# A fused attention and MLP kernel: q and k of batch 1 released by half of w_in's third quarter, w_out by the first 256 keys, and another searched order of all instructions

## The chip, the cores and the metric

The kernel runs on one core of a Trainium2 chip. The metric is the time of one execution on the device, in microseconds (us). A core has five engines with a stream of instructions each: TensorE (PE, matrix products; PEld are its weight loads), VectorE (DVE), ScalarE (ACT), GpSimd (POOL) and SyncE (SP, which here only issues transfers). Transfers (DMA) issued by SP, POOL and ACT run on 16 DMA engines that all queues share. Working memory is SBUF; matrix products land in PSUM, in 8 banks.

## The reference

```python
def _attn_ref(q, k, v, global_idx):          # q, k, v: 8 batches, 8 heads, 576 positions, 64
    scores = scale * np.matmul(q, k.transpose(0, 1, 3, 2))
    mask = np.abs(pos[:, None] - pos[None, :]) <= 32
    mask = mask | is_global[:, None] | is_global[None, :]      # 8 global positions
    scores = np.where(mask, scores, -1000000000.0)
    attn = np.exp(scores - np.max(scores, axis=-1, keepdims=True))
    return np.matmul(attn / (np.sum(attn, axis=-1, keepdims=True) + 1e-09), v)

def _moe_ref(x, w_in, w_out):                # 4608 tokens, 512 -> 2048 -> 512
    h = x @ w_in
    g = np.maximum(h, 0.0) + np.log1p(np.exp(-np.abs(h)))     # softplus
    return g @ w_out
```

The second function takes the first one's output, with the heads of a position side by side, as x.

## The kernel before

A batch's 576 positions are 18 blocks of 32. The unit of attention is a *pair* n (36 in all): four blocks of 32 queries, all 8 heads. A query block sees its own and the two neighbouring key blocks, and a slot with the 8 global keys. For pair n the steps are: scores `s` (L1085, 64 small matmuls), for the first four pairs on top of a mask that a full-size matmul puts into PSUM (L1068, L1078); row maximum `m` (L1100 or L1102, VectorE); exponential `st` (ScalarE, L1121 or L1125); sum and reciprocal `rs` (L1134, VectorE); multiplication `pn` (L1140, GpSimd or VectorE); transposition into `pt` (L1149, VectorE). The 8 global queries of a batch are computed apart: `sg` scores, `gm` and `gnb` maxima, `pg` exponential, `pgt` its transpose, `ov` values, `vg` the result.

Four pairs are a tile m of 512 tokens (9 tiles). Its values `xo` (L1259) are products of `pt` with `vb`; they are copied to `xT` (L728). Then `h` = xT times w_in (L1294, 16 column groups c of 128, 4 matmuls each), softplus `g` (L1300, ScalarE), and `o` = g times w_out (L1305), which is copied to `osb` and stored. The first tile's values come in three groups of 1, 2 and 1 pairs, the second tile's in two (1 and 3), so that h starts early on 128 and 256 columns.

Batches 0 and 1 come in naturally: for q and for k two *parts* of 256 positions (512 KB each) and a small part of 64 positions in two transfers. Each part is cast to bf16 (`qb`, `kb`), transposed on TensorE (`tr`, L865 or L868, with a product that picks the global rows, L871 or L875), and copied into `qx` and `kx`. Later batches are loaded in another layout and transposed on VectorE.

SP issues q, k and (from batch 1 on) v in one queue. POOL issues batch 0's v (8 transfers `vb`), w_in (`win`: four quarters, each in two halves of 64 partitions, 8 transfers), w_out (`wout`, 4 transfers) and the stores. Since SP's transfers would start at once, SP first issues a tiny transfer that reads one element of a weight tile, so that it waits until that weight has landed: `follow` (L761, tile `trail`). Ahead of batch 1's parts it reads the last partition of w_in's third quarter, which its second half brings. In the same way a one-column copy `seen` on GpSimd (L1373, L1437) holds w_in and w_out back until a part has landed.

The order of everything is set by a planner in the file, the class `_Order`. Each job has a cost per engine, dependencies, PSUM banks. The planner walks through `ORDER`, a table of numbers (job times 5 plus engine) that a search outside the file has found, and emits the jobs in the order of the times that its own model gives. This model also contains the fetching of TensorE's instructions in blocks (`BLOCK = 256`, asked for at instruction 130 and every 256 later, needed at 448 and every 256 later: `ASK`, `NEED`, `stall`), the DMA queues (`settle`), a price for going from one TensorE tile shape to another (`SWITCH`, job attribute `array`), and fills waits of TensorE in the first 34 us with matmuls that nobody reads (`keep`, `warm`, L737).

## Time and profile before

| what | value |
|---|---|
| three runs | 333.17, 333.18, 332.8 us; median 333.17 |
| the profiled execution | 331.16 us, its span on the core 329.1 us |
| mean granted TensorE clock | 0.995 |
| instructions in the span | 12101 |
| busy | PE 97%, PEld 52%, DVE 67%, ACT 71%, POOL 60% |
| chain that ended last | PE 90%; o 39%, h 37% |
| read / written from memory | 36.71 MB / 9.44 MB |

The profiled execution is one; its own time is 2 us under the median of the three. Busy shares are shares of the span; a matmul's end is modelled, so a busy PE is not PE at its peak. In a row of the order of time, the first number is the start in us from the span's start, the second the time from the first instruction's start to the last one's end, xN the number of instructions, and in brackets the idle time ahead of them with what ended it.

### The profile page before, as it was taken

The page shows a single profiled execution, that of the slowest core. Times are in us where ns is not written, and L with a number is a line of the kernel's source. Part 1 is how long each engine was busy: PE and PEld are TensorE (multiplying, and loading weights), DVE is VectorE, ACT ScalarE, POOL GpSimd, SP SyncE. Part 2 cuts the span into 40 slices and gives each one's busy share as a digit, 9 for nine tenths or more (in the row PEclk, how much of TensorE's full clock was granted, in tenths as well). Part 3 has the DMA queues.
Part 4 walks back from the last instruction along what each step waited for, and adds up shares of the span by engine and source line. Part 5 has one row for each costly group of instructions (what it writes and reads, how often), then busy time and mean ns, then how long its engine had stood idle before and what let it go on. Part 6 is the DMA issues. An engine that isn't in the chain of part 4 may idle for free.

```text
span 329.1 us, 12101 instructions
## 1 busy us (share of the span) xinstructions
PE 319.9 (97%) x5290; PEld 171.3 (52%) x5290; DVE 219.9 (67%) x386; ACT 233.8 (71%) x459; POOL 196.0 (60%) x175
## 2 busy tenths in 40 slices
PE   8878999999999999999999999999999999999996
PEld 3536876565555444544555445445544454454444
DVE  7796689847997799884995975378776970431000
ACT  5698879676798896488558857995749647914622
POOL 7827828996678567969587496738282927230000
PEclk9997999999999999999999999999999999999999
DMA  7998999999889899999999960370010012001002
GB/s 193 187 205 195 198 189 155 157 166 244 136 152 146 152 226 173 180 228 189 178 179 167 155 162 4 127 145 3 4 66 0 36 66 85 13 32 66 34 32 97
DMA packets 168796, 42.14 MB, mean 128 GB/s; under 512 B 153256, under 2 KB 165800, under 8 KB 168744
## 3 DMA queue, kind: packets, MB, share of 16 engines
q1 hardware_dynamic: 155928, 27.15, 46.8%
q0 software_dynamic: 10944, 11.08, 16.9%
q10 hardware_dynamic: 1872, 3.15, 2.5%
q8 instruction: 41, 0.67, 0.9%
q14 instruction: 11, 0.09, 0.1%
HBM read 36.71 MB, written 9.44 MB: 140 GB/s over the span
## 4 chain that ended last, share of the span: by engine, by line
PE 90%; DVE 2%; SPq 2%; DMA 2%; issue 1%; ACT 1%
PE o L1305 39%; PE h L1294 37%; PE xo L1259 4%; PE s L1085 4%; DMA stage<-in_q_dram 2%; PE ov L1005 2%; SPq L522 1%; PE pick L894 1%; SPq L526 1%; PE sg L976 1%; PE warm L737 1%; DVE qx L728 1%; PE tr L865 1%; DVE m L1100 1%; PE pick L907 1%
## 5 line engine op out<-in xcount | busy, mean ns | idle before, releaser
L1305 PE MATMUL o<-wout,g 128*128 128x512 bf16 (+1 forms) x592 | 138.3, 374 | 0.0
L1294 PE MATMUL h<-xT,win 128*128 128x512 bf16 (+3 forms) x768 | 137.8, 328 | 0.1
L1300 ACT ACTIVATE g<-h 128x512 bf16<-128x512 f32 (+3 forms) x192 | 84.5, 503 | 30.0 <-PE h L1294 27.0
L1140 POOL TENSOR_TENSOR pn<-st,rs 128x1024 bf16<-128x1024 f32 (+1 forms) x38 | 66.7, 1766 | 55.7 <-DVE rs L1134 49.9
L1294 PEld LDWEIGHTS <-win 128*128 128x128 bf16 x768 | 67.5, 99 | 59.6 <-issue 0.8
L1305 PEld LDWEIGHTS <-g 128*128 128x128 bf16 x592 | 55.9, 98 | 60.7 <-ACT g L1300 1.0
L1108 POOL TENSOR_TENSOR st<-st,m 128x1024 f32<-128x1024 f32 x32 | 60.2, 1894 | 27.1 <-DVE m L1102 27.0
L1089 DVE TENSOR_TENSOR st<-s,mask 128x512 f32<-128x512 f32 x64 | 41.1, 677 | 18.6 <-PE s L1085 18.4
L1132 DVE TENSOR_REDUCE sm<-st 128x8 f32<-128x1024 f32 x32 | 38.5, 1203 | 14.8 <-ACT st L1125 14.6
L1102 DVE TENSOR_REDUCE m<-st 128x8 f32<-128x1024 f32 x32 | 37.9, 1209 | 0.3
L728 ACT COPY osb<-o 128x512 f32<-128x512 f32 (+1 forms) x30 | 17.2, 577 | 22.6 <-PE o L1305 20.2
L1125 ACT ACTIVATE st<-st 128x1024 f32<-128x1024 f32 x32 | 32.7, 1052 | 0.3
L1149 DVE STREAM_TRANSPOSE pt<-pn 128x512 int32<-128x512 int32 x36 | 24.5, 690 | 5.2 <-POOL pn L1140 5.1
L728 ACT CAST xT<-xo 128x512 bf16<-128x512 f32 (+3 forms) x28 | 11.7, 467 | 18.8 <-PE xo L1259 18.8
L728 DVE CAST xT<-xo 128x512 bf16<-128x512 f32 (+3 forms) x20 | 11.3, 601 | 17.5 <-PE xo L1259 17.4
L1300 ACT ACT_TABLE_LOAD x15 | 19.2, 1283 | 1.7 <-PE h L1294 1.5
L1125 ACT ACT_TABLE_LOAD x14 | 18.0, 1283 | 0.7 <-ACT osb L728 0.4
L725 POOL TENSOR_SCALAR qb<-stage 128x1152 bf16<-128x1152 f32 (+2 forms) x15 | 16.8, 1126 | 2.2 <-issue 1.1
L1085 PE MATMUL s<-kx,qx 64*32 64x128 bf16 x1152 | 14.5, 220 | 3.6 <-issue 2.8
L1085 PEld LDWEIGHTS <-qx 64*32 64x32 bf16 x1152 | 10.4, 90 | 12.2 <-issue 8.9
L728 POOL CAST vb<-stage 128x1152 bf16<-128x1152 f32 x12 | 13.7, 1146 | 3.3 <-DMA stage<-in_v_dram 3.3
L737 PE MATMUL warm<-vb 128*128 128x512 bf16 x46 | 13.9, 451 | 1.3 <-DVE vb L559 1.3
(127 smaller groups left out, 287.2 us busy)
## 6 DMA issues: line engine op xcount, KB each, us to landing
stage<-in_v_dram SPq DMA_DIRECT2D x56, 144.0 KB, 4.2
stage<-in_q_dram SPq DMA_DIRECT2D x48, 144.0 KB, 3.7
stage<-in_k_dram SPq DMA_DIRECT2D x48, 144.0 KB, 4.0
out_dram<-osb POOLq DMA_DIRECT2D x24, 256.0 KB, 3.2
out_dram<-osb ACTq DMA_DIRECT2D x11, 256.0 KB, 2.0
stage<-in_q_dram SPq DMA_DIRECT2D x4, 512.0 KB, 6.2
stage<-in_k_dram SPq DMA_DIRECT2D x4, 512.0 KB, 6.9
win<-in_moe_w_in_dram POOLq DMA_DIRECT2D x8, 256.0 KB, 7.7
```

What stands on the lines that cost most here:

```text
L728: {"ACT": nc.scalar.copy, "DVE": V.tensor_copy, "POOL": nc.gpsimd.tensor_copy}[e](out, in_)
L1085: nc.tensor.matmul(out=PS["s", n, g][quad(a), x, :], lhsT=qx[b % 2][rows(g), a, j * BL:(j + 1) * BL], rhs=kx[b % 2][rows(g), a, e0 * BL:(e ...
L1089: V.tensor_tensor(out=PS["st", n][:, h, :, :], in0=PS["s", n, h][:, :, :], in1=mask[:, h, j0:j0 + PB, :, :].rearrange("p j s i -> p j (s i ...
L1102: V.reduce_max(out=m[:], in_=flat(PS["st", n], h0, h1), axis=AX)
L1108: on(e).tensor_tensor(out=t, in0=t, in1=over(PS["m", n, y][:], SL * BL), op=OP.subtract)
L1125: nc.scalar.activation(out=t, in_=t, func=AF.Exp)
L1132: V.reduce_sum(out=sm[:], in_=flat(PS["st", n], h0, h1), axis=AX)
L1140: on(e).tensor_tensor(out=PS["pn", n][:, :, :, h0:h1].rearrange("p x s h -> p h x s"), in0=PS["st", n][:, h0:h1], in1=PS["rs", n, y][:].re ...
L1149: V.transpose(out=bass.AP(base.tensor, base.offset, ap=[list(base.ap[0]), [2 * STEP, PB // 2], [STEP + BL // 2, 2], [1, SL * BL]]), in_=PS ...
L1294: nc.tensor.matmul(out=h[:, :], lhsT=w_in_t[c // 4][:, kd, c % 4 * P:(c % 4 + 1) * P], rhs=PS["xT", m][:, kd, lo:hi], start=(kd == 0), sto ...
L1300: nc.scalar.activation(out=PS["g", m, c][:, lo:hi], in_=PS[key][:, lo_of(c, hi - lo)], func=AF.Softplus)
L1305: nc.tensor.matmul(out=PS["o", m, ns, a][:, :], lhsT=PS["g", m, kf][:, ns * P:(ns + 1) * P], rhs=w_out_t[kf // 4][:, kf % 4, a:z], start=( ...
```

## The change

It has four parts. `follow` gets the row that it reads: for w_in row 0, which the first half of the third quarter brings, and batch 1's parts depend on that half alone. The `seen` copy ahead of w_out waits for the first 256 keys of batch 1, where it waited for the next 256. The hold times of w_in and w_out on GpSimd go (they only shift the planner's times). And the planner's constants are others (SWITCH, SLOW, BEGIN, the fills, the latency of a POOL transfer; `array` numbers that count the changes between the score, value and global shapes), with a table `ORDER` searched anew under them. Its rows tell a reader nothing; two stand here.

```diff
-    SWITCH = 107
+    SWITCH = 96
-    SLOW = ((27000, 8000), (34500, 6200), (55000, 8200), (230000, 6000), (1e9, 4500))
+    SLOW = ((27000, 6500), (36500, 5500), (50000, 7500), (230000, 5800), (1e9, 4500))
-                took_ = max(next(x for until, x in self.SLOW if ask < until), self.backlog(ask + 1200) - ask + 2400)
+                took_ = max(next(x for until, x in self.SLOW if ask < until), self.backlog(ask + 1400) - ask + 2400)
-    BEGIN = 3300
+    BEGIN = 2900
-                dma.append((mine, t + 1500 if j["cost"][e][0] else t, j["moves"], j))
+                dma.append((mine, t + (1900 if mine == "POOL" else 1500) if j["cost"][e][0] else t, j["moves"], j))
-    ORDER = (52, 57, 62, 162, 167, 122, 137, 146, 156, 4, 117, 113, 151, 141, 132, 127, 182, 172, 177, 187, 370, 9, 14, 213,
+    ORDER = (52, 156, 146, 113, 141, 151, 57, 162, 62, 167, 127, 9, 132, 137, 122, 4, 211, 215, 226, 258, 243, 245, 260, 230,
...
-    def follow(x, t):
+    def follow(x, t, row):
-        nc.sync.dma_start(out=trail[x:x + 1, :], in_=t[D:D + 1, t.shape[1] - 1, t.shape[2] - 2:])
+        nc.sync.dma_start(out=trail[x:x + 1, :], in_=t[row:row + 1, t.shape[1] - 1, t.shape[2] - 2:])
-                    follow(0, w_in_t[2])
+                    follow(0, w_in_t[2], 0)
-            T["part", b, w, t] = o.add({"DMA": (700 if b else 0, 0)}, emit, had(("w_in", 2)) + T["cast", 0, w] if b else [], rank=0,
+            T["part", b, w, t] = o.add({"DMA": (700 if b else 0, 0)}, emit, had(("w_in", 2, 0)) + T["cast", 0, w] if b else [], rank=0,
-                             rank=3, array=32, ins=16 * n, ...   # ov
+                             rank=3, array=34, ins=16 * n, ...
-                         rank=1, array=64, urgent=last is None, ...   # val
+                         rank=1, array=65, urgent=last is None, ...
-            last = T["w_in", x] = o.add({"POOL": (650, 0)}, lambda e, x=x, y=y: weights_in(x, y), [last or T["held"]],
-                                        rank=-1 if x else 0, hold=2000 if x else 0, moves=1340)
+            last = T["w_in", x] = T["w_in", x, y] = o.add({"POOL": (650, 0)}, lambda e, x=x, y=y: weights_in(x, y), [last or T["held"]],
+                                        rank=-1 if x else 0, moves=1340)
-            T["landed"] = o.add(pool(100), lambda e: nc.gpsimd.tensor_copy(seen[:, 0, :], natural(1, 1)[:, 0, 0, 0, 0:1]), [T["part", 1, 1, 1]], rank=0)
+            T["landed"] = o.add(pool(100), lambda e: nc.gpsimd.tensor_copy(seen[:, 0, :], natural(1, 0)[:, 0, 0, 0, 0:1]), [T["part", 1, 1, 0]], rank=0)
-                                      [T["landed"], T.get(("w_out", a - 1))], rank=-1, hold=800 if a else 0, moves=2700)
+                                      [T["landed"], T.get(("w_out", a - 1))], rank=-1, moves=2700)
```

What the new table does with the order is seen at three places. The first is SP's queue from its start: stage_60 is where q lands, stage_61 k, stage_62 v; 128x8x128 is a part of 256 positions, 64x4x64 half of a small one. Before:

```order
L531 DMA gi<-in_global_idx_dram 128x16
L522 DMA stage_60<-in_q_dram 128x8x128
L522 DMA stage_61<-in_k_dram 128x8x128 x2
L522 DMA stage_60<-in_q_dram 128x8x128
L526 DMA stage_61<-in_k_dram 64x4x64 x2
L526 DMA stage_60<-in_q_dram 64x4x64 x2
L765 DMA trail<-win_126 1x2x1
L522 DMA stage_61<-in_k_dram 128x8x128 x2
L526 DMA stage_60<-in_q_dram 64x4x64 x2
```

After:

```order
L531 DMA gi<-in_global_idx_dram 128x16
L522 DMA stage_61<-in_k_dram 128x8x128
L522 DMA stage_60<-in_q_dram 128x8x128
L522 DMA stage_61<-in_k_dram 128x8x128
L526 DMA stage_61<-in_k_dram 64x4x64 x2
L526 DMA stage_60<-in_q_dram 64x4x64 x2
L522 DMA stage_60<-in_q_dram 128x8x128
L765 DMA trail<-win_126 1x2x1
L522 DMA stage_61<-in_k_dram 128x8x128 x2
L522 DMA stage_60<-in_q_dram 128x8x128
```

The first keys go ahead of the first queries, batch 0's second 256 queries behind the four small transfers, and batch 1's first queries ahead of its small parts.

The second is GpSimd's queue at the loads of v (vb_66) and w_in (win_124 to win_127 are its four quarters). Before:

```order
L725 TENSOR_SCALAR qb<-stage_60 128x2x4x64
L477 DMA vb_66<-in_v_dram 32x18x64 x8
L1373 COPY seen<-stage_60 128x1
L1356 DMA win_124<-in_moe_w_in_dram 64x4x512 x2
L671 COPY mask<-mask 128x2x256
L1356 DMA win_125<-in_moe_w_in_dram 64x4x512 x2
L1356 DMA win_126<-in_moe_w_in_dram 64x4x512 x2
L1356 DMA win_127<-in_moe_w_in_dram 64x4x512 x2
L1140 TENSOR_TENSOR pn<-st,rs 128x512 x6
```

After:

```order
L728 CAST kb<-stage_61 128x2x4x64 x2
L477 DMA vb_66<-in_v_dram 32x18x64 x4
L725 TENSOR_SCALAR qb<-stage_60 128x256
L477 DMA vb_66<-in_v_dram 32x18x64 x4
L1373 COPY seen<-stage_60 128x1
L1356 DMA win_124<-in_moe_w_in_dram 64x4x512 x2
L1356 DMA win_125<-in_moe_w_in_dram 64x4x512 x2
L1356 DMA win_126<-in_moe_w_in_dram 64x4x512 x2
L1356 DMA win_127<-in_moe_w_in_dram 64x4x512
L1140 TENSOR_TENSOR pn<-st,rs 128x512 x2
L1356 DMA win_127<-in_moe_w_in_dram 64x4x512
```

A cast of the small query part now stands between the two halves of v, and two pn multiplications stand ahead of w_in's last half.

The third is VectorE between batch 0's last query cast and the transpose of the global exponentials (pgt), where TensorE waits for the copies qx_68. Before:

```order
L723 TENSOR_SCALAR qb<-stage_60 128x256
L1100 TENSOR_REDUCE m<-s 128x4 x2
L728 CAST qg_72<-pick 64x4x8 x2
L728 COPY qx_68<-tr 128x4x128
L1100 TENSOR_REDUCE m<-s 128x4
L982 TENSOR_REDUCE gm<-sg 128x1 x2
L983 TENSOR_REDUCE gnb<-gm 128x1
L728 COPY qx_68<-tr 128x4x128
L675 TENSOR_TENSOR own<-posM,gf 128x9x2x8
L993 STREAM_TRANSPOSE pgt<-pg 128x160
```

After:

```order
L723 TENSOR_SCALAR qb<-stage_60 128x2x4x64
L1100 TENSOR_REDUCE m<-s 128x4 x2
L728 CAST qg_72<-pick 64x4x8 x2
L1100 TENSOR_REDUCE m<-s 128x4
L982 TENSOR_REDUCE gm<-sg 128x1 x2
L983 TENSOR_REDUCE gnb<-gm 128x1
L1134 RECIPROCAL rs<-sm 128x4
L675 TENSOR_TENSOR own<-posM,gf 128x9x2x8
L728 COPY qx_68<-tr 128x4x64
L1134 RECIPROCAL rs<-sm 128x4
L1100 TENSOR_REDUCE m<-s 128x4
L728 COPY qx_68<-tr 128x4x128
```

The cast is now one of a large part, and the last large qx copy moves behind the maxima of the next pair and two reciprocals.

On TensorE, 21 fill-in matmuls open the program in place of 29, and 43 in all in place of 46. The mask matmuls of pair 0 (L1068) stand behind the transposes of k, not ahead of them. Behind the first value group, 48 h matmuls come, then two fill-ins, then four h of the last quarter of w_in and the second value group; before, 60 h, three fill-ins and that group. The other matmuls are the same ones in another order.

More of the change, by code (lines that the diff above doesn't have):

```diff
@@ L154 @@
     WARM = 0
-    FILL, FILLT, NARROW, NFILL, NFILLT = 0.75, 220, 0, 0.8, 140
-    COLD, COLDT, LONG = 5400, 427, 0.93
+    FILL, FILLT, NARROW, NFILL, NFILLT = 0.75, 220, 0, 0.93, 57
+    COLD, COLDT = 5400, 427
     STARVE = 900
@@ L172, in keep @@
         if t0 < self.COLD:
-            span = (t1 - t0) * self.LONG
+            span = (t1 - t0) * 0.93
             cold = min(span, self.COLD - t0)
@@ L775, in add_load @@
                     last = T["half", 0, h] = o.add({"POOL": (1300, 0)}, lambda e, h=h, x=x: load_v(nc.gpsimd, 0, h, range(2 * x, 2 * x + 2)), [last], rank=0,
-                                                   moves=1200, late=200)
+                                                   moves=1080, late=200)
                     T["cast", 0, 2].append(last)
@@ L782, in emit @@
                     if behind:
-                        follow(1, w_out_t[0])
+                        follow(1, w_out_t[0], D)
                     load_v(nc.sync, b, h, range(R))
@@ L795, in emit @@
                 if b:
-                    follow(0, w_in_t[2])
+                    follow(0, w_in_t[2], 0)
                 load_part(b, w, t)
-            T["part", b, w, t] = o.add({"DMA": (700 if b else 0, 0)}, emit, had(("w_in", 2)) + T["cast", 0, w] if b else [], rank=0,
-                                       moves=(1800 if b else 1900) if t < FULL else 900 if b else 650, units=1 if t < FULL else 2)
+            T["part", b, w, t] = o.add({"DMA": (700 if b else 0, 0)}, emit, had(("w_in", 2, 0)) + T["cast", 0, w] if b else [], rank=0,
+                                       moves=1800 if t < FULL else 900 if b else 650, units=1 if t < FULL else 2)
     def add_cast(b, w):
@@ L1042, in add_global @@
             ovs.append(o.add({"PE": (72 * n, 72 * n + 170) if b else (110 * n + 100, 110 * n + 240)}, lambda e, m0=m0, m1=m1: ov(e, m0, m1), [tps[-1], *ovs, *T["cast", b, 2]],
-                             rank=3, array=32, ins=16 * n, opens=[] if ovs else [("ov", ("ov", b, y)) for y in range(two)], uses=[("ov", b, y) for y in range(two)] if ovs else []))
+                             rank=3, array=34, ins=16 * n, opens=[] if ovs else [("ov", ("ov", b, y)) for y in range(two)], uses=[("ov", b, y) for y in range(two)] if ovs else []))
         T["gexp", b], T["tpg", b], T["ov", b] = exps[-1], tps[-1], ovs[-1]
@@ L1275, in add_values @@
             last = o.add({"PE": (t, t + 170)}, lambda e, s0=s0, s1=s1: val(e, s0, s1), ready if last is None else [last] + (had(("gv", 0)) if ahead else []),
-                         rank=1, array=64, urgent=last is None, ins=16 * (s1 - s0) + (8 if ahead and s0 == 0 else 0), opens=opened if last is None else [],
+                         rank=1, array=65, urgent=last is None, ins=16 * (s1 - s0) + (8 if ahead and s0 == 0 else 0), opens=opened if last is None else [],
                          uses=[("pt", m)] + ([("xo", v_, r) for r in range(KD)] if last is not None else []))
```

142 rows, old and new, of the table ORDER are left out of this document.

## The prediction

> **What bounds the kernel now.** I read the page first (busy times, then the slices with the granted clock), then TensorE's waits, then the busy time by stretch, and only then the order of time of the first 46 us. The first two lines are of the page, the third of TensorE's waits (total, times, longest).
>
> ```profile
> PE 319.9 (97%) x5290; PEld 171.3 (52%) x5290; DVE 219.9 (67%) x386; ACT 233.8 (71%) x459; POOL 196.0 (60%) x175
> PEclk9997999999999999999999999999999999999999
> PE s L1085 <- issue: 2.8, 1, 2.8
> ```
>
> TensorE is the bound, and its clock falls once, in the fourth slice. By stretch (columns: length, busy time of PE, PEld, DVE, ACT, POOL, granted clock, DMA share, GB/s):
>
> ```profile
> 16.00:24.00 8.00, 6.63 (x204) 3.54 (x202) 7.82 (x23) 7.53 (x40) 2.41 (x4) 1.00 1.26 206
> 24.00:26.00 2.00, 0.00 (x0) 0.00 (x0) 1.46 (x5) 2.00 (x13) 0.48 (x1) 1.00 1.15 190
> 28.00:30.00 2.00, 2.00 (x19) 1.80 (x18) 0.86 (x3) 2.00 (x13) 1.56 (x2) 0.53 1.03 299
> 46.00:100.00 54.00, 53.92 (x1112) 32.58 (x1110) 43.87 (x70) 42.87 (x95) 42.84 (x29) 1.00 0.96 170
> 100.00:200.00 100.00, 100.00 (x1820) 50.06 (x1819) 80.91 (x127) 73.42 (x112) 74.24 (x53) 1.00 0.96 175
> ```
>
> From 46 us on TensorE has no gap, so what the front of the program wins or loses arrives at the end one for one, and any instruction added later costs its length. The front, TensorE in order of time:
>
> ```profile
> 1.26 8.76 PE L737 MATMUL warm<-vb 128*128 128x512 bf16 x29 [1.26 <-DVE vb L559]
> 10.67 0.39 PE L865 MATMUL tr<-ident,kb 128*128 128x128 bf16 x4
> 17.39 0.43 PE L976 MATMUL sg<-kx,qg 128*32 128x320 bf16 x8
> 20.03 0.44 PE L1085 MATMUL s<-kx,qx 64*32 64x128 bf16 x32 [0.38 <-DVE qx L728]
> 22.89 0.41 PE L1085 MATMUL s<-kx,qx 64*32 64x128 bf16 x30
> 26.14 0.23 PE L1085 MATMUL s<-kx,qx 64*32 64x128 bf16 x2 [2.84 <-issue]
> 26.30 0.48 PE L1245 MATMUL xo<-vb 128*128 128x128 bf16 x4
> 28.20 4.33 PE L1294 MATMUL h<-xT,win 128*128 128x128 bf16 x60
> 32.36 0.81 PE L737 MATMUL warm<-vb 128*128 128x512 bf16 x3
> 33.10 0.43 PE L1259 MATMUL xo<-pt,vg 32*64 32x256 bf16 x8
> ```
>
> The 32 score matmuls of block 3 break after 30, and the wait has no releaser ("issue"). Counted from the program's start, the break is at instruction 704, which is 448 + 256, the place at which the planner's own NEED and BLOCK expect a fetched page of instructions. So I read it as TensorE waiting for its next page. The 60 h matmuls behind it last 4.33 us, 72 ns each, with the clock at 0.53.
>
> **The change, part by part.** *Front.* The table now loads k's first part ahead of q's, and the last 256 queries of batch 0 behind the small parts; the first transposes stand ahead of the mask matmuls; 21 fill-in matmuls open the program, not 29. These rows carry the chain that follows:
>
> ```profile
> 7.35 1.14 ACT L728 CAST kb<-stage 128x512 bf16<-128x512 f32 x2 [1.18 <-DMA stage<-in_k_dram]
> 9.18 1.14 ACT L728 CAST kb<-stage 128x512 bf16<-128x512 f32 x2 [0.69 <-DMA stage<-in_k_dram]
> 15.07 0.39 DVE L723 TENSOR_SCALAR qb<-stage 128x256 bf16<-128x256 f32 x1 [0.22 <-DMA stage<-in_q_dram]
> 15.41 1.29 DVE L1100 TENSOR_REDUCE m<-s 128x4 f32<-128x512 f32 x2
> 18.35 0.81 DVE L982 TENSOR_REDUCE gm<-sg 128x1 f32<-128x320 f32 x2
> 19.26 0.72 DVE L728 COPY qx<-tr 128x512 bf16<-128x512 bf16 x1
> 20.09 0.35 DVE L993 STREAM_TRANSPOSE pgt<-pg 128x160 int32<-128x160 int32 x1
> 22.96 0.72 DVE L1140 TENSOR_TENSOR pn<-st,rs 128x512 bf16<-128x512 f32 x1
> 24.60 0.71 DVE L1149 STREAM_TRANSPOSE pt<-pn 128x512 int32<-128x512 int32 x1
> ```
>
> Eight fill-ins fewer at 0.22 us let the transposes start near 8.2, when the second large part (landed by 7.35, one cast of 0.6) is there; before, 10.67. But the last query part is now the last transfer of its queue: VectorE and ScalarE both stand in line for its cast, the row maxima and exponentials queued behind them. It cannot land before 9.18 + 1.8 (one large part, 7.35 to 9.18) + 1.2 for the four small ones = 12.2, nor after 15.07, the last landing now; four instead of eight v transfers compete, so I take 12.8. VectorE is then free at 13.1. From there its order is cast 0.6, two maxima 1.3, two small copies 0.4, a maximum 0.65, the global maxima 0.95, two reciprocals and own 0.65, a half copy 0.4, a maximum 0.65, the qx copy 0.7: 6.3 us, so block 2's scores start at 19.4 against 20.03. Of 2.5 us won on TensorE, 0.6 are left. Then pgt 1.1, pn 0.7, two maxima 1.3, three small ones 0.3, pt 0.7: block 0 is transposed at 23.5, and its value matmuls run then, if instructions are there; before, 26.30, which the page of instructions set (pt stood ready at 25.3).
>
> *The page.* It is asked for some 320 instructions ahead, by the planner's ASK, at instruction 386: the last of the sg group, which I put at 15.8 (before, in the scores ahead of 17.39, and the page was usable at 26.14, 8.9 us later). What it stood behind:
>
> ```profile
> 6.17 5.59 POOL L477 DMA_DIRECT2D vb<-in_v_dram  x8
> 12.31 0.64 POOL L1356 DMA_DIRECT2D win<-in_moe_w_in_dram  x1 [0.35 <-DMA vb<-in_v_dram]
> 14.73 3.68 POOL L1356 DMA_DIRECT2D win<-in_moe_w_in_dram  x6
> 25.30 0.73 SPq L765 DMA_DIRECT2D trail<-win  x1
> 25.52 4.04 POOL L1140 TENSOR_TENSOR pn<-st,rs 128x512 bf16<-128x512 f32 x4 [7.11 <-DVE rs L1134]
> stage<-in_q_dram SPq DMA_DIRECT2D x48, 144.0 KB, 3.7
> out_dram<-osb POOLq DMA_DIRECT2D x24, 256.0 KB, 3.2
> win<-in_moe_w_in_dram POOLq DMA_DIRECT2D x8, 256.0 KB, 7.7
> ```
>
> At 206 GB/s (stretch 16 to 24) a w_in transfer of 256 KB takes 1.27 us of the DMA engines. By 17.2 six were issued (12.31, 13.57, then from 14.73 at 0.61 each). GpSimd now holds back the second four v transfers for a cast of the small query part (lands about 10.4), so w_in starts near 13.8, and by 15.8 four are issued. Two fewer ahead are 2.5 us: 8.9 - 2.5 = 6.4 after 15.8, usable at 22.2; with a page's own length of slack I take 23.3. That is just under 23.5, so this step gains the stall and costs nothing new; the cover is 0.2 us thin.
>
> *Quarter four.* h then starts at 23.5 + 1.9 (28.20 - 26.30) = 25.4 at full clock: 48 matmuls at 0.056 end at 28.1. Now the last 12 to 16 wait: w_in's last half is issued behind two pn multiplications, the second of which waits for a VectorE reciprocal at about 22; issue at 23.1. A POOL transfer of 256 KB takes 3.2 us to land when little is in the queue and 7.7 among w_in; 26.3 to 30.8, and since only two w_in stand ahead, but k's parts join, 28.5. The second value group follows at 29.05, where before it stood at 33.10: -4.05. Eight h matmuls are still owed: 8 x 0.056 = +0.45.
>
> *Behind it.* Before, transposes of batch 1 filled the time in which the new xT is evicted; now four fill-ins do: +1.3 (xT copies of 0.4 on two engines behind the table load and softplus). Fill-ins elsewhere (46 to 43) lie in waits and cost nothing by themselves.
>
> *Switches.* By TensorE's order, visits to the small tile shapes rise from 45 to 52. One visit's price:
>
> ```profile
> 77.84 0.82 PE L1294 MATMUL h<-xT,win 128*128 128x384 bf16 x4
> 78.59 0.37 PE L907 MATMUL pick<-place,picked 128*32 128x8 bf16 x32
> 75.70 1.30 PE L1294 MATMUL h<-xT,win 128*128 128x384 bf16 x7
> 76.84 0.38 PE L1305 MATMUL o<-wout,g 128*128 128x512 bf16 x1
> ```
>
> Seven h ahead of a full-size matmul take 1.14 us, 0.163 each; four ahead of a small one take 0.75, 0.10 more than four times that. Going in costs 0.10; coming out is between nothing and another 0.18 (half the 0.37 of a small group). Seven at 0.18 are +1.25 (0.7 to 2.0).
>
> *q, k and w_out earlier.* trail leaves SP one w_in transfer sooner, about 24.0 for 25.30, and w_out is gated by the first keys. Neither is first needed when it lands: TensorE's order has 28 h matmuls of 256 columns (twice 0.056 each, 3 us) and the third value group ahead of batch 1's first transposes, so nothing is gained or lost; if that cover fails, the block-4 and block-5 scores are late next, by up to 1 us. By its order, ScalarE has four activation-table loads fewer; it is 71% busy: nothing.
>
> Sum: -4.05 + 0.45 + 1.3 + 1.25 = -1.05 us. The profiled execution (331.16) would become 330.1; the runs' median is 333.17, 2.0 above it, and I carry the difference over: 332.1.
>
> By the Trainium skill, "DMA: Bandwidth & Descriptors", Queues, rings and completion order, each DMA engine takes turns between the queue rows that have work. By that rule a page on a queue of its own does not wait for all that was issued before it, and fewer w_in ahead would not help. By the Trainium skill, "Runtime: NRT & Kernel Launch", Instruction fetch mechanics, crossing a block of 256 instructions is mostly hidden; the 2.84 us of this trace, exactly at such a place, say otherwise here.
>
> **The rivals.** *The page takes 8.9 us wherever it is asked for* (a turn-taking queue, as the rule above has it). Asked at 15.8 it is usable at 24.7, the value group is 1.2 later; w_in's last half hides half of that, val group two at 29.65: -0.45 in all, 332.7. For it speaks only that one page cannot tell a queue's length from a constant. Chance 0.13, with the late last w_in half (30.8 at worst) that lands in the same place.
>
> *Stall kept, slower.* The page comes when w_in's stream lets it, as before at about 26.1. Then the value group is at 26.3, h at 28.2 at half clock, the second value group near 32.4: -0.7, and the additions of 0.45, 1.3 and 1.25 stay: +2.3, 335.4. It decides from a page later than about 25.5. For it: the DMA share of 1.26 and 206 GB/s are the transfers' own limit, and TensorE now asks at a time when the same queue is just as full; the later pages (instructions 960 and 1216) come 3 to 4 us sooner too. Against it: fewer are issued ahead. Chance 0.23.
>
> *More gained.* w_in's last half lands as early as before (28), the xT gap is filled to 0.45, a visit costs 0.10: -4.6 + 0.45 + 0.45 + 0.7 = -3.0, 330.2. For it: VectorE, which I charge with every step in line, is the weak link of my chain, and a landing at 12.2 frees it sooner. Chance 0.22.
>
> **How the numbers follow.** My forecast, 332.1, has the remaining 0.42. Its own range is 331.2 to 333.2. A change under 0.2% (0.67 us, about what a measurement of this kernel can tell from none) begins at 332.5; I give 0.28 of the 0.42 to faster and 0.14 to the same. So faster 0.28 + 0.22 = 0.50, the same 0.14 + 0.13 = 0.27, slower 0.23. The range reaches from the larger gain's 330.0 to the kept stall's 335.4.
>
> **What would show it.** After: no wait "issue" above 0.5 us on the score line, and the clock full past 16 us; first transposes near 8.2; block 2's scores at 19 to 20; h from about 25.4; a break in h of up to 0.5 us at its last quarter; the second value group near 29; then about 1.3 us of fill-in and gap ahead of the 256-column h; from 46 us no waits. A wait "issue" of 1 us or more anywhere in the first 45 us, with a clock under 0.9, would make the prediction wrong; so would VectorE reaching block 2 after 20.5, or TensorE waits behind 46 us.

## The result and the profile after

The changed kernel is slower: 344.7 us median of four runs (341.6 to 347.21), before 332.99 us (330.82 to 333.18), ratio 1.0336 with a 95% interval of 1.0249 to 1.0423. Some executions, of any kernel, run some per cent longer at a lower clock; the ratios leave them out (here the one of 347.21), the medians do not, and both profiles of section 10 are of such ones. The forecast was 332.1 with a range of 330.0 to 335.4. The profiled execution took 341.6 us with a span of 339.8, against 331.16 and 329.1 before, so there are 10.7 us to find in the two traces.

Busy times and granted clock from the page, then TensorE's waits (total, times, longest), in the kernel after:

```profile
PE 316.8 (93%) x5243; PEld 171.0 (50%) x5287; DVE 222.1 (65%) x390; ACT 233.6 (69%) x456; POOL 190.6 (56%) x170
PEclk9999999997999999989999999999999999999999
```

```profile
PE xo L1259 <- issue: 6.0, 3, 2.4
PE h L1294 <- DVE xT L728: 2.7, 1, 2.7
```

TensorE fell from 97% of the span to 93%. A part of that is no idle time: 44 of after's 5287 matmuls have no record, though their weight loads have. Before, the clock dipped once, early; now it dips in the 10th and the 18th slice, which is far behind the front. The first row holds three waits for instructions, the second one wait for a copy by VectorE. The stretches:

```profile
16.00:24.00 8.00, 6.35 (x158) 3.24 (x157) 7.04 (x22) 7.79 (x40) 5.47 (x9) 1.00 1.17 174
24.00:26.00 2.00, 0.15 (x26) 0.15 (x33) 0.00 (x0) 1.01 (x6) 0.94 (x1) 1.00 1.24 202
28.00:30.00 2.00, 2.00 (x39) 2.00 (x37) 0.98 (x4) 1.98 (x11) 1.65 (x3) 1.00 0.99 277
46.00:100.00 54.00, 50.02 (x920) 29.17 (x927) 47.56 (x76) 40.70 (x90) 34.70 (x24) 0.97 0.95 167
100.00:200.00 100.00, 95.62 (x1687) 48.54 (x1702) 79.77 (x123) 72.86 (x109) 68.97 (x50) 0.98 0.90 164
```

From 46 to 100 us TensorE is busy 50.02 of 54.00, where it was 53.92; from 100 to 200 it is 95.62, where it was 100.00. The front, TensorE in order of time:

```profile
8.33 0.40 PE L865 MATMUL tr<-ident,qb 128*128 128x128 bf16 x4 [1.04 <-ACT qb L721]
19.70 0.42 PE L1085 MATMUL s<-kx,qx 64*32 64x128 bf16 x32 [0.45 <-DVE qx L728]
23.56 0.21 PE L1259 MATMUL xo<-pt,vb 32*64 32x64 bf16 x2
25.85 0.48 PE L1259 MATMUL xo<-pt,vb 32*64 32x64 bf16 x38 [2.08 <-issue]
27.24 2.85 PE L1294 MATMUL h<-xT,win 128*128 128x128 bf16 x48
30.68 0.32 PE L1259 MATMUL xo<-pt,vg 32*64 32x256 bf16 x8
```

The wait for the instruction page has only moved from the score line to the first value group, 2.08 us long where it was 2.84. The late waits, with what stands before two of them:

```profile
73.35 1.67 PE L1305 MATMUL o<-wout,g 128*128 128x512 bf16 x7 [0.16 <-issue]
77.77 1.41 PE L1294 MATMUL h<-xT,win 128*128 128x384 bf16 x4 [2.75 <-DVE xT L728]
...
140.71 0.70 PE L1259 MATMUL xo<-pt,vb 32*64 32x64 bf16 x60
143.85 0.43 PE L1259 MATMUL xo<-pt,vb 32*64 32x96 bf16 x28 [2.45 <-issue]
...
274.11 1.16 PE L1259 MATMUL xo<-pt,vb 32*64 32x32 bf16 x117
276.72 0.22 PE L1259 MATMUL xo<-pt,vb 32*64 32x64 bf16 x3 [1.46 <-issue]
```

I split each trace at the start of the 64th `o` matmul (L1305), which lies behind the front. (It is counted by the weight loads, since 30 of after's 592 `o` matmuls have no record. Ahead of it both kernels do the same matmuls, but for 46 and 43 fill-ins.) To there, before takes 70.31 us and after 70.28. From there to the end of the span it is 258.77 and 269.54, a loss of 10.77. So the 10.7 us between the two traces are lost behind the front, where I had forecast "no waits".

Why VectorE was late at 77.77 (VectorE, then GpSimd, in order of time):

```profile
71.33 1.30 DVE L596 TENSOR_SCALAR place<-pos,pi 128x32 bf16<-128x32 f32 x1
72.99 4.14 DVE L601 TENSOR_TENSOR pick<-posK,gf 32x144 bf16<-32x144 f32 x4
77.16 1.49 DVE L728 CAST xT<-xo 128x384 bf16<-128x384 f32 x3
```

```profile
70.69 1.90 POOL L1140 TENSOR_TENSOR pn<-st,rs 128x1024 bf16<-128x1024 f32 x1 [0.40 <-ACT osb L728]
73.18 1.50 POOL L725 TENSOR_SCALAR qb<-stage 128x1152 bf16<-128x1152 f32 x1
74.58 1.49 POOL L728 CAST kb<-stage 128x1152 bf16<-128x1152 f32 x1
```

`make_pick`, a small job that is done once, builds the table `pick` with four comparisons (L601). The new order moved it from 39 to 71 us. The same line in the trace of before, then of after (min/median/max ns, first and last start):

```profile
L601 DVE TENSOR_TENSOR pick<-posK,gf x4: 296/302/620, 40.1 to 41.3; 32x144 bf16<-32x144 f32 x4
```

```profile
L601 DVE TENSOR_TENSOR pick<-posK,gf x4: 297/302/3193, 73.0 to 76.8; 32x144 bf16<-32x144 f32 x4
```

One comparison that takes 0.30 us alone took 3.19 (72.99 to 76.18), and it ended just behind GpSimd's two casts (73.18 to 76.07). The step before it, L596, ran 1.30 us (0.12 before), to the end of GpSimd's `pn`. Before, only one short cast of GpSimd met the comparisons, and one of them took 0.62. By the Trainium skill, "SBUF — State Buffer", Who interferes with whom, a VectorE instruction with two SBUF inputs contends with a GpSimd instruction that reads SBUF. This trace agrees (3.19 against 0.30 us), and the xT copies that TensorE waited for stood behind it.

### The profile page after: what moved, and what is told of

Read it like the earlier page. It is cut to its first block, busy times and chain, and to the rows that moved or that the text cites. A ratio compares the mean times of both kernels' runs of the same rounds, so it can differ in the third digit from the quotient of the medians.

```text
span 339.8 us, 12043 instructions
## 1 busy us (share of the span) xinstructions
PE 316.8 (93%) x5243; PEld 171.0 (50%) x5287; DVE 222.1 (65%) x390; ACT 233.6 (69%) x456; POOL 190.6 (56%) x170
## 4 chain that ended last, share of the span: by engine, by line
PE 84%; DVE 5%; issue 4%; ACT 2%; SPq 2%; DMA 2%; POOL 1%; ACTq 0%; POOLq 0%
PE h L1294 36%; PE o L1305 34%; PE xo L1259 4%; PE s L1085 3%; DMA stage<-in_q_dram 2%; PE ov L1005 2%; ACT st L1121 1%; PE pick L894 1%; DVE pick L601 1%; SPq L526 1%; SPq L522 1%; PE sg L976 1%; PE warm L737 1%; DVE sm L1132 1%; POOL pn L1140 1%
## 5 line engine op out<-in xcount | busy, mean ns | idle before, releaser
L1305 PE MATMUL o<-wout,g 128*128 128x512 bf16 (+1 forms) x562 | 133.0, 375 | 3.3 <-issue 2.7
L1294 PEld LDWEIGHTS <-win 128*128 128x128 bf16 x768 | 66.4, 98 | 62.8 <-issue 5.9
L1140 POOL TENSOR_TENSOR pn<-st,rs 128x1024 bf16<-128x1024 f32 (+1 forms) x39 | 67.9, 1750 | 52.4 <-DVE rs L1134 47.3
L1305 PEld LDWEIGHTS <-g 128*128 128x128 bf16 x592 | 56.0, 98 | 61.6 <-ACT g L1300 1.2
L728 ACT COPY osb<-o 128x512 f32<-128x512 f32 (+1 forms) x29 | 16.5, 574 | 27.1 <-PE o L1305 24.9
L728 ACT CAST xT<-xo 128x512 bf16<-128x512 f32 (+3 forms) x24 | 11.0, 512 | 16.1 <-PE xo L1259 16.1
L1259 PE MATMUL xo<-pt,vb 32*64 32x96 bf16 (+2 forms) x1328 | 14.5, 211 | 6.0 <-issue 6.0
L1259 PEld LDWEIGHTS <-vb 32*64 32x64 bf16 x1328 | 13.8, 103 | 7.5 <-issue 7.0
L725 POOL TENSOR_SCALAR qb<-stage 128x1152 bf16<-128x1152 f32 (+2 forms) x11 | 12.9, 1173 | 3.7 <-DMA stage<-in_q_dram 2.4
```

What stands on the lines that cost most here:

```text
L728: {"ACT": nc.scalar.copy, "DVE": V.tensor_copy, "POOL": nc.gpsimd.tensor_copy}[e](out, in_)
L1140: on(e).tensor_tensor(out=PS["pn", n][:, :, :, h0:h1].rearrange("p x s h -> p h x s"), in0=PS["st", n][:, h0:h1], in1=PS["rs", n, y][:].re ...
L1259: nc.tensor.matmul(out=PS["xo", v_, c][h * D:(h + 1) * D, (x - X0) * BL:(z - X0) * BL], lhsT=lhs, rhs=rhs, start=start and not ahead, stop ...
L1294: nc.tensor.matmul(out=h[:, :], lhsT=w_in_t[c // 4][:, kd, c % 4 * P:(c % 4 + 1) * P], rhs=PS["xT", m][:, kd, lo:hi], start=(kd == 0), sto ...
L1305: nc.tensor.matmul(out=PS["o", m, ns, a][:, :], lhsT=PS["g", m, kf][:, ns * P:(ns + 1) * P], rhs=w_out_t[kf // 4][:, kf % 4, a:z], start=( ...
```

## The experiments

Three theories were tried. *Hold*: the late xT wait is `make_pick` held by GpSimd. *Page*: the late waits named issue come from where the requests for instruction pages fall in the program; the trace records each page as one 16 KB packet on its queue for instructions, so the start of each fetch is known. *Named part*: the rival that the early q, k and w_out cost something. All numbers in the table are of the profiled executions but the last two columns. The medians of before are those of the sessions in which the others ran.

| kernel | to the 64th o | from there to the end | median | ratio to before |
|---|---|---|---|---|
| before | 70.31 | 258.77 | 332.8 to 333.4 | 1 |
| after | 70.28 | 269.54 | 344.7 | 1.0336 [1.0249, 1.0423] |
| 1 pick early | 74.72 | 265.37 | 341.62 | 1.0256 [1.0205, 1.0306] |
| 2 split waits | 74.65 | 264.66 | 340.93 | 1.0215 [1.0153, 1.0277] |
| 3 GpSimd waits | 75.00 | 264.64 | 341.81 | 1.0231 [1.0179, 1.0283] |
| 4 both, 1 and 2 | 72.25 | 260.88 | 335.5 | 1.0094 [1.0057, 1.013] |
| 5 both, old gates | 74.65 | 259.80 | 336.76 | 1.0108 [1.0068, 1.0148] |
| 6 before, pick late | 70.00 | 260.38 | 335.91 | 0.9998 [0.9954, 1.0041] |
| 7 before, named part | 75.09 | 258.79 | 335.95 | 1.0077 [1.0042, 1.0111] |
| 8 before, +60 instructions | 74.55 | 265.09 | 342.32 | 1.0288 [1.0248, 1.0327] |
| 9 before, +256 instructions | 76.01 | 258.80 | 335.16 | 1.006 [1.0027, 1.0092] |

The column "to the 64th o" needs care. TensorE's granted clock falls to one half for whole stretches of 3.41 us in the front, and how many of them a front gets changes from run to run: in the profiled runs after had none there, before, 4, 6, 8 and 9 had one, 2, 3, 5 and 7 had two, 1 had three. At half clock for 3.41 us, TensorE loses at most 1.7 us of work. Kernels 4 and 2, whose fronts hold the same matmuls, differ by one such stretch and by 74.65 - 72.25 = 2.4 us; kernel 2 also has a wait of 0.88 us at 52.35 that kernel 4 does not have. I compare fronts with the same number only.

### 1. The pick job back at 41 us

```diff
 ORDER:
-... 1942, 197, ...
+... 762, 812, 197, 1810, ...
```

> The changed kernel with one piece of VectorE's work, the building of the constant pick (L595 to L603), put back from about 71 us to about 41 us, where GpSimd is idle. Theory 'three separate late waits': TensorE's 2.75 us wait for xT at 75 us goes, with the half clock behind it; the changed kernel's span of 339.8 us becomes 334.9 (-4.9), and the two waits at 141 and 275 us stay. Rival 'VectorE is late everywhere': the same 2.3 us of work done earlier only moves the wait; a TensorE wait of 2 us or more stays within 20 us of the old place and the span is within 1.5 us of 339.8.

The xT wait at 77.77 is gone, and the four comparisons take what they take alone:

```profile
L601 DVE TENSOR_TENSOR pick<-posK,gf x4: 297/299/304, 44.3 to 45.3; 32x144 bf16<-32x144 f32 x4
```

From the 64th to the 100th `o` TensorE needs 21.31 us, after 25.89, before 20.86. The two late issue waits stay (2.64 and 1.73). The span did not fall, since this run's front had three half-clock stretches and after's none; from the 64th `o` to the end 4.17 us are won. The place of the pick job is a cause; the profiled span alone would have hidden it.

### 2. One small matmul ahead of two value groups

```diff
+                if v_ in TOUCH:          # TOUCH = (6, 10)
+                    nc.tensor.matmul(out=PS["xo", v_, 0][0:D, 0:BL], lhsT=idle[quad(0), 0, 0:D], rhs=run(0, 0, X0, SELF[0], []), start=True, stop=True)
```

The groups at 140 and 274 us wait for several producers. In these traces no weight load or matmul of TensorE carries more than one wait (421 of after's carry one); what is left over stands ahead of the group as a wait instruction of its own, and TensorE's sequencer, which hands out its instructions, stands at that. Here such an instruction stands 266 (and 252) instructions ahead of the next page's first one; it was passed at 139.43 (273.19), the fetch began at 141.31 (274.39), and the group reached the page's start 1.4 us after its first matmul (139.98 to 141.41, 273.88 to 275.26). The extra matmul takes some of the waits, so that the rest fit on instructions and nothing stands alone.

> The changed kernel with one small matmul more (32 columns, weights of zeros, into a bank that the next matmul overwrites) ahead of the value groups at 140 and 274 us. TensorE's program then waits for pt in an ordinary instruction and no longer in a separate wait instruction. Theory 'TensorE's sequencer stands at the separate wait and so asks for its next page late': the pages are fetched 3 us or more ahead of their need, the waits of 2.45 and 1.46 us and the half clock at 144 us go, span 339.8 - 5.9 = 333.9 us. Rival 'the page stands behind other transfers': the fetches start as late as before, the waits stay, span 339.8.

```profile
PE h L1297 <- DVE xT L729: 2.8, 1, 2.8
PE o L1308 <- issue: 2.5, 16, 0.2
PE s L1086 <- issue: 0.9, 1, 0.9
PE xo L1262 <- issue: 0.5, 1, 0.5
```

(TensorE's waits behind 46 us; the added lines shift the numbers, L1262 is L1259 of after.) The second row is no wait: at these 16 places an `o` matmul has no record, while its weight load has; the same row comes back in 4 and 8. The waits of 2.45 and 1.46 us on the value groups are down to 0.5 and nothing. The page of the first group is fetched from 144.06 and the group starts at 144.37; that of the second is fetched from 272.22, and the group starts at 274.98. The wait of 0.9 us on a page, at 52.35, lies in the front and is not of this edit: kernel 3, whose matmuls are those of after, has 0.88 at 52.69. From the 64th `o` on 4.88 us are won. The xT wait stays, as it should.

### 3. GpSimd held behind the pick job

```diff
+                if (b, w, e) == (2, 0, "POOL"):
+                    nc.gpsimd.tensor_copy(seen[:, 0, :], pick[:, 0, 0, 0:1])
```

> The changed kernel in which GpSimd, behind pn at 70.7 us, copies one column of pick before it scales q, so that it does not run while VectorE builds pick; VectorE's order is as in the changed kernel. Theory 'VectorE's pick waits for GpSimd, not for its own work': the four pick operations take 1.2 to 1.6 us in all where they took 4.14, the xT wait falls from 2.75 to under 0.5 us, no half clock, span about 335.5 us. Rival 'the 2.3 us of work itself, in the wrong place': pick takes 4.1 us again, the wait stays above 1.5 us, span above 338.5 us.

GpSimd now reads one column of `pick` before it scales q, so its casts start behind the first comparisons. VectorE's group, and the wait that follows on TensorE:

```profile
77.72 2.40 DVE L601 TENSOR_TENSOR pick<-posK,gf 32x144 bf16<-32x144 f32 x4
```

```profile
80.75 1.41 PE L1296 MATMUL h<-xT,win 128*128 128x384 bf16 x4 [1.01 <-DVE xT L728]
```

The order of the jobs is that of after; only GpSimd's start moved. The comparisons fall from 4.14 to 2.40 us and the wait from 2.75 to 1.01. A last comparison of 1.44 us still met a cast, so the wait did not vanish. That the time follows GpSimd's start, with VectorE's own order untouched, is what tells the hold by GpSimd from a VectorE that merely had too much to do. The 4.90 us that this row of the table gains from the 64th `o` on are not all of this edit: the half-clock stretches that after has at 79.06 and 143.92 are both missing here, though the wait for the page at 145 us is still 2.24.

### 4. Both together

The edits of 1 and 2.

> The changed kernel with pick put back to 41 us and the two small matmuls ahead of the value groups at 140 and 274 us, so both edits that each took away their own wait. If the three late waits are independent and are all of the late loss: behind 46 us no TensorE wait of 1 us or more, and from the 64th to the 562nd matmul of the second layer 253 us (before 251.95, after 261.34). The front is as in the changed kernel: 2 us of wait near 24 us, and half a clock behind it in some executions (0, 3.4 or 6.8 us of it). Span 329 to 333 us. Rival 'each repair opens another wait': 1 us or more of wait at a new place behind 46 us, and 256 us or more for that stretch.

```profile
PE o L1308 <- issue: 2.5, 16, 0.2
PE s L1086 <- DVE kx L729: 1.2, 1, 1.2
PE xo L1262 <- issue: 0.6, 1, 0.6
```

The two gains add up: 8.66 us from the 64th `o` on, where 4.17 + 4.88 = 9.05. The ratio falls from 1.0336 to 1.0094. So these two causes are most of the loss; 0.94% above before remains. Of the 2.11 us that are left from the 64th `o` on, the two waits shown are 1.8: a new one of 1.17 for `kx` at 82.39, which the expectation had ruled out, and 0.62 that is left of the first group's.

### 5. Both, with the old gates

```diff
-                    follow(0, w_in_t[2], 0)
+                    follow(0, w_in_t[2], D)
-            ... natural(1, 0)[:, 0, 0, 0, 0:1]), [T["part", 1, 1, 0]], rank=0)
+            ... natural(1, 1)[:, 0, 0, 0, 0:1]), [T["part", 1, 1, 0]], rank=0)
```

> After, with the pick job back at 41 us and the two small matmuls ahead of value groups 6 and 10 (335.5 us, ratio 1.0094), and now also the named part undone: trail reads the second half of w_in's third quarter and w_out is gated by the next 256 keys, as in before; the order is still that of after. Theory A (the early q and k cost through the DMA queues in any order, as they did in before, +2.6): 333 to 334. Theory B (the searched order has given these transfers their place, and the rest is the front's own work): 335 to 336.5, the same as without the undoing within 0.3%. Theory C (the order counts on the early arrival): slower than 336.5, with a wait for batch 1's transposes or w_out between 30 and 46 us.

336.76 against 335.5, with intervals that overlap: in after's order, undoing the named part changes nothing that these runs can tell. From the 64th `o` on this run is 1.08 us shorter than kernel 4, its front 2.4 us longer with one more half-clock stretch. The two waits that kernel 4 had left are 0.43 and 0.33 us here; whether the gates do that stays open.

### 6. The kernel before, with the pick job at 70 us

```diff
 ORDER:
-... 770, 776, 197, 922, ...
+... 2256, 1897, 197, 2075, ...
```

> The kernel before with one thing changed: VectorE builds pick behind its transposes at 69.7 us, where it stands idle for 3.67 us until the next xT, instead of at 39 us. Theory 'two of VectorE's operations are held while GpSimd runs': GpSimd is busy from 68.8 to 75.2 us without a gap of note, so pick ends only near 75, xT is 1.5 to 2.5 us late, TensorE waits 1 to 2.5 us near 75 us, with or without half a clock behind it (another 1.7): span 329.1 + 1 to 4. Rival 'only the work counts': 2.3 us of work fit into 3.67 us of idle time, no wait, span 329.1 within 0.7 us.

```profile
L601 DVE TENSOR_TENSOR pick<-posK,gf x4: 304/1450/1644, 70.3 to 74.9; 32x144 bf16<-32x144 f32 x4
```

Three of the four comparisons are held (4.89 us in all), TensorE waits 1.41 for xT, and from the 64th `o` on 1.61 us are lost. But the ten runs fell into two groups (four from 331 to 333, six from 335 to 338, where the thirteen of before lie between 331.2 and 334.8), and the ratio is 1. The hold is shown, its cost in the kernel before is not: whether the upper group comes of the hold stays open.

### 7. The kernel before, with the named part alone

```diff
-        nc.sync.dma_start(out=trail[x:x + 1, :], in_=t[D:D + 1, t.shape[1] - 1, t.shape[2] - 2:])
+        nc.sync.dma_start(out=trail[x:x + 1, :], in_=t[(0, D)[x]:(0, D)[x] + 1, t.shape[1] - 1, t.shape[2] - 2:])
-            ... natural(1, 1)[:, 0, 0, 0, 0:1]), [T["part", 1, 1, 1]], rank=0)
+            ... natural(1, 0)[:, 0, 0, 0, 0:1]), [T["part", 1, 1, 1]], rank=0)
```

> The kernel before with the named part of the change alone: the small transfer that opens SP's queue for q and k of batch 1 reads a row of the first half of w_in's third quarter instead of the second, and w_out is gated by the first 256 keys. The order of all engines is that of the kernel before. Theory 'the loss is in the order, not in the transfers': within 0.7 us of the kernel before (span 329.1), first keys land 1 us sooner. Rival 'earlier transfers make TensorE's pages late': the pages needed at 33 to 48 us land up to 1.3 us later; with their slack of 1.2 to 3 us there, a wait of up to 1 us and 330 us.

```profile
38.65 1.59 PE L1294 MATMUL h<-xT,win 128*128 128x256 bf16 x13 [1.37 <-issue]
45.94 0.21 PE L868 MATMUL tr<-ident,qb 64*64 64x64 bf16 x1 [1.59 <-issue]
```

Slower by 0.77%. Two page fetches that began at 32.94 and 36.74 before begin at 36.20 and 43.55, and TensorE waits for two pages that it had in time. Behind the 64th `o` nothing is lost (258.79 against 258.77). From 26 to 28 us the DMA engines are full here (share 1.02, before 0.35), since batch 1's parts start earlier. So in this order the earlier q, k and w_out are not free: what they meet there is the fetching of instructions.

### 8. and 9. The kernel before, with 60 and with 256 instructions more

For 8, fill-in matmuls between 12 and 19.5 us are replaced by four times as many narrow ones; for 9, the 29 wide ones that open the program by 157 narrow ones. The order stays nearly the same. So does TensorE's time in 8; in 9 the narrow ones take 10.95 us and the wide ones took 8.76.

```diff
 # 8
-        thin = t0 < self.NARROW
+        thin = 12000 < t0 < 19500
-        for x in range(n):
+        for x in range(4 * n + 0 if thin else n):
 # 9
+        thin = n > 20
-        for x in range(n):
+        for x in range(n + 128 if thin else n):
```

> The kernel before with the 10 fill-in matmuls between 13 and 19 us (512 columns) turned into 40 of 128 columns, the same time, but 60 instructions more ahead of the scores at 20 us. Theory 'the page is asked for late, because TensorE's program stands at a wait': asked for ahead of that wait, the page lands in time, the 2.84 us at 23.3 us and the half clock behind it (1.7) go or shrink to under 1 us; span 329.1 - 3 to - 4.5 = 325 to 326. Rival 'a page takes 8 us or more while w_in streams': the stall comes earlier in the score work and is as long, span 329.1 within 1 us.

> The kernel before, with its opening 29 wide fill-in matmuls replaced by 157 narrow ones (128 columns in place of 512): TensorE gets exactly 256 instructions more, one whole page, and every later instruction keeps its place within its page. Theory A (the place within the page decides): no wait named issue of 1 us or more behind 46 us, from the 64th o matmul on the times stand as in before (o64 to the last: 251.95 us, within 0.5), and the whole is 333 to 335. Theory B (more instructions cost by themselves, as a share of each page or of the queue): with four times the added instructions of the shift by 60 the new waits are as many as there (seven) or more and the time is 342 or above.

TensorE's waits behind 46 us, first with 60 more, then with 256 more:

```profile
PE h L1294 <- issue: 2.9, 3, 2.6
PE o L1305 <- issue: 2.8, 17, 0.2
PE xo L1259 <- issue: 2.2, 1, 2.2
PE s L1085 <- issue: 2.1, 1, 2.1
```

```profile
PE o L1306 <- issue: 1.0, 1, 1.0
PE tr L869 <- issue: 0.8, 1, 0.8
```

A wait of 1.77 us at 144.10 in the first, which the view puts down to a copy by ScalarE, stands at the start of a page too; with it, the waits behind the 64th `o` are 6.0 of the 6.3 us lost there (the one of 2.6 us lies ahead of it). The wait at 23.3 us, which kernel 8 was to remove, became two of 1.51 and 1.96 us, both at page starts. Sixty more cost 9.5 us; four times as many, which leave each later instruction at its place within its page of 256, cost 0.6%, some 2 us, no more than the longer opening, and from the 64th `o` on the traces of before and of 9 take 258.77 and 258.80 us. The place within the page decides, not the number of instructions. The kernel before stands well in its pages, and any edit that adds or takes instructions in the front moves every page boundary behind it. The two waits that are left (1.0 and 0.8) lie in the front, so the expectation of none behind 46 us held only behind the 64th `o`.

### 10. The new order shifted, with and without the early pick

For the kernel after, 12 fill-ins became 54 narrow ones (84 instructions more), once as it is and once with the edit of 1.

```diff
+        thin = 15000 < t0 < 18000
+        for x in range(4 * n + 6 if thin else n):
```

> The changed kernel with its 12 fill-in matmuls at 16 us (512 columns) turned into 54 of 128 columns: nearly the same time (54 x 0.055 = 3.0 us for 12 x 0.22 = 2.6 us, into a wait of 0.45 us), but 84 instructions more, so every later instruction stands 84 places further on in its page. Theory 'it is the place in the page that decides': the two separate waits at 140 and 274 us now stand 176 and 162 instead of 266 and 252 instructions ahead of the next page, the pages are asked for before them, and the waits of 2.45 and 1.46 us with the half clock at 144 us go (-5.9); the page that was needed at 23.8 us is asked for before the scores' wait at 19.7 us and no longer stalls (-2.1). The wait for xT at 75 us stays. Span 339.8 - 8 = 332, at worst 334 if the first page still stalls. Rival 'the transfers decide': pages are as late as before, waits stay, span 339.8 or up to 1 us more.

> The same shift of 84 instructions, and pick built at 41 us as in the run with pick put back. All four waits should then be gone: 339.8 - 8 - 4.9 = 327 us of span, 328.5 us, some 1.5% faster than the kernel before. Rival 'a kernel with this front cannot keep its gain': a new wait of 2 us or more turns up and it ends no faster than the kernel before (331 to 335 us).

The medians are 351.99 and 347.16 us, the ratios 1.0442 [1.0393, 1.049] and 1.0351 [1.0293, 1.0409], on two runs each. The waits at 141 and 275 us are gone in both, but six others of 1.4 to 2.9 us come in the first kernel and seven of 1.0 to 2.3 in the second. Moving the pages cured the two places and hurt others. The ratios differ by 0.9%, about what the edit of 1 gained in the kernel after (0.8%).

### 11. w_in spread out, or held back

The first kernel issues w_in's transfers 3 to 6 behind the first `pn` of GpSimd and the last behind the second; the next also holds the third until block 2's queries are copied (and tells the planner so, which leaves out ten fill-ins); the last adds the edits of 1 and 2 (the matmul ahead of group 7 too).

```diff
 ORDER:
+... 398, 83, 88, 93, 98, ... 453, 103, ...
+        if (x, y) == (1, 0):
+            nc.gpsimd.tensor_copy(seen[:, 0, :], qx[0][:, 0, 2 * P:2 * P + 1])
+            nc.gpsimd.tensor_copy(seen[:, 0, :], qx[0][:, 0, 2 * P + 1:2 * P + 2])
```

> The changed kernel in which GpSimd issues w_in's transfers 3 to 6 behind its first pn (18.7 us) and the seventh behind its second, so that two instead of four of them stand ahead of the page of instructions that is needed at instruction 704. Theory 'the page waits behind the transfers issued before it is asked for': its fetch starts by 21.0 us instead of 23.3, the wait of 2.08 us at 23.8 us goes, span 1.5 to 2 us shorter (338). Rival 'a page takes its 9 to 10 us while the queue is full, whatever was issued': it starts at 23.3 again, the wait stays, span within 0.7 us of 339.8 or longer by the four fill-ins more (0.9 us).

> The changed kernel in which GpSimd copies two columns of the queries of block 2 (written at 19.6 us) before it issues w_in's third transfer, so nothing of w_in but the first two transfers is issued before TensorE's program passes its wait for the same queries at 19.7 us. Theory 'the first page is asked for when that wait ends, and then stands behind what is in the queue': with the queue short it starts 1.2 to 2 us behind 19.9, so at 21 to 22 instead of 23.3, and the wait of 2.08 us falls to under 0.7 us. Rival 'it is asked for at 16 us and takes 7': it starts at 23.3 again. w_in's later transfers land about 1 us later. Ten fill-in matmuls fewer follow from the changed times, so all later pages are cut 20 instructions earlier, and the waits behind 46 us may stand elsewhere; only the front is read.

> All repairs in one: pick at 41 us, small matmuls ahead of three value groups, and w_in's third transfer behind block 2's queries. If nothing new turns up, 339.8 - 4.9 - 5.9 - 1.5 = 327.5 us of span (329 us), 1% faster than the kernel before. Rival: the pages, cut 20 instructions earlier than in the changed kernel, fall into another dense group, with a new wait 'issue' of 1.4 to 3 us behind 34 us for each page whose request stands less than about 4 us ahead of its need; 331 to 337.

Ratios 1.0348 [1.0296, 1.0399], 1.0467 [1.0419, 1.0516] and 1.0214 [1.0158, 1.027]. Spread out, w_in still streams from 18.75 us on, and the front's page is fetched from 23.44 as in after (23.31), although the DMA engines had room at 20 to 21 us (share 0.68, in after 1.21): no change. Held back, the fetch begins at 21.48 and the first value group no longer waits, but now w_in is late (TensorE in the second kernel):

```profile
27.15 4.28 PE L1294 MATMUL h<-xT,win 128*128 128x128 bf16 x48 [2.10 <-DMA win<-in_moe_w_in_dram]
33.12 0.38 PE L1294 MATMUL h<-xT,win 128*128 128x128 bf16 x4 [1.69 <-DMA win<-in_moe_w_in_dram]
```

What the page gains the weights lose, 2.10 + 1.69 against 2.08. The last kernel has such waits too (2.31, 0.56 and 1.78). I found no version that beats the kernel before.

## Why the prediction was wrong

- **The chain to the first value group** was right: first transposes at 8.33 for 8.2, block 2's scores at 19.70 for 19.4, first value matmuls of pt at 23.56 for 23.5.
- **The page** failed. I had it asked at 15.8 and usable at 23.3; it was usable at 25.85, so h came at 27.24 for 25.4 and the second value group at 30.68 for 29.05. The step that failed is the time of asking, which I took from the planner's ASK. The fetch began at 23.31, which is 3.40 us after TensorE's sequencer got past its next wait instruction, behind the scores of block 2 that held it (19.91); before, 23.83 and 20.21, so 3.62; with the DMA engines nearly idle (second kernel of 11, share 0.08 from 21 to 22 us) 21.48 and 20.51, so 0.97. No trace records the request itself. But nothing in them shows one at 15.8, and the first kernel of 11, where the engines had room at 20 to 21 us and the fetch still began at 23.44, speaks against one that merely stood in the queue. That both the later request and the full queue cost is my reading of these starts. The rival "Stall kept, slower" named the mechanism: it decided from 25.5, and 25.85 is just behind that. Its price of 335.4 has nothing of the late waits either.
- **"From 46 us no waits"** is the step that cost most, and it was no term of my sum at all. I read the order only up to 46 us and took the rest to be free because it was full before. It cost 10.77 us of the profiled span. The new order put the pick job beside GpSimd's casts (2.75 us of wait and a half-clock stretch; 4.17 undone) and two value groups so that a page starts 252 to 266 instructions behind a wait of their own (2.45 and 1.46 and a half-clock stretch; 4.88 undone). The sign that I had named for being wrong, waits behind 46 us, is what came.
- **The visits to small tile shapes**, +1.25 (0.7 to 2.0), fit but are not shown apart: with both causes and the gates undone (kernel 5), 1.03 us remain from the 64th `o` on.
- **The q, k and w_out step at nothing** was wrong in the order of before, where it costs 0.77%, and cannot be told from nothing in the order of after. Its premise failed too: `trail` was to leave SP at 24.0 for 25.30 and left at 25.49, and the first w_out transfer at 35.84 for 35.89, because this order sends w_in later (from 14.32 for 12.31). So the changed kernel issues batch 1's keys no earlier than before (26.32 for 26.14); the gate alone, in the order of before, brings `trail` to 23.72. I asked only who needs the data, not what their transfers take the place of: the page fetches.
- **The front's gain** did not come. With one half-clock stretch in both, kernel 4 reaches the 64th `o` at 72.25, before at 70.31: 1.94 us later, where I had the front 2.3 us ahead (4.05 less 0.45 less 1.3). Some of this is the page. The 65th `h` starts at 34.90 in kernel 4 and at 35.64 before, but before has by then done 32 matmuls of batch 1's keys more (34.34 to 35.64, 1.30 us), so kernel 4 is not ahead there. Behind it, kernel 4 waits 0.45 us for `kb` and 0.44 for `qx`, before 0.20 in all. The rest stays open.

## What to carry to other kernels

When an order is searched anew, compare the whole of it, every engine from end to end, for small jobs that have moved: a 0.3 us VectorE operation can take 3 us beside GpSimd, and a planner that prices it as a constant will put it there. A program whose TensorE stream is long has page boundaries as part of its tuning; before judging any change that alters the instruction count early on, repeat it with filler that makes up a whole page of 256 instructions, and find the fetches in the trace. And cut the trace at a landmark behind the front, so that clock stretches of the front do not hide or fake what a change does later.

## What the runs showed of the hardware

- A VectorE comparison held beside GpSimd takes as long as the GpSimd work that stands in the way: 0.30 us became 0.62 to 3.19. The held ones ended 0.10 to 0.16 us behind the end of a GpSimd instruction (76.18 behind 76.07 in after; 80.11 behind 80.00 in 3; 71.97, 73.44 and 74.90 behind 71.82, 73.34 and 74.80 in 6; 40.99 behind 40.83 before).
- A page of 256 TensorE instructions is fetched as one packet of 16 KB. In the sixteen traces TensorE waits 55 times for 0.5 us or more without a releaser, and each time at the start of a page, and until 2.2 to 3.0 us after that page's packet began. The stand-alone waits 251 to 266 instructions ahead of a page were followed by its fetch 1.2 to 1.9 us later, in before as in after (254 and 251 ahead: 1.59 and 1.38 us; 266 and 252: 1.88 and 1.20). In before these cost nothing, since what stood between ran longer than the fetch; the two value groups of after reached the page in 1.4 us. By the Trainium skill, "Runtime: NRT & Kernel Launch", Instruction fetch mechanics, the blocks are 16 KiB of 256 instructions and crossing into one is mostly hidden; the runs agree with the first, and against the second stand these waits of 0.5 to 3.6 us.
- The granted clock falls in steps of 3.413 us: every half-clock stretch in these traces is that long or twice as long (but for those cut off by the end of the span), and where the steps begin differs from one execution to the next. A gap can cost such a stretch (after, 2.75 us at 75.02 and 2.45 at 141.41) or none (after, 2.08 us at 23.77), which makes up to 1.7 us (half of 3.413) between two runs of one kernel.
